# The 64-row step of the products with w_in on both halves of the PE array

## The chip, the cores and the metric

The kernel runs on one core of one Trainium2 chip. The metric is the device time of one execution in microseconds (us). Its engines are PE (TensorE, matmul), DVE (VectorE), ACT (ScalarE), POOL (GpSimd) and SP (SyncE, which issues most DMAs here); each works through its own list of instructions in order.

## The reference

A transformer block in float32: 2048 tokens, width 448, attention with 16 heads of 28, then a gated MLP with spatial mixing. The change lies in the second half:

```python
h = _layernorm(x) * (1 + cb) + sb          # 2048 x 448
z = _gelu(h @ w_in)                        # 448 -> 1792
z1 = z[..., :896]
z2 = _layernorm(z[..., 896:])
g = w_sp @ z2 + b_sp[:, None]              # w_sp 2048 x 2048
x = x + gb * ((z1 * g) @ w_out)            # w_out 896 x 448
```

## The kernel before

All large products use values split into a high and a low part: high = the value rounded to the PE's fast 32-bit format, low = the rest, and a product is high x high + high x low + low x high. The contraction over 448 is cut into three chunks of 128 rows and one of 64. Operands are kept as slots: 0 to 2 are the high parts of the three chunks, 3 to 5 the low parts. The last chunk needs only 64 rows, so its slot 6 holds the high part in rows 0 to 63 and, on the activations' side, the low part in rows 64 to 127; on the weights' side slot 6 holds the high part twice. One full step (6, 6) thus gives high x high and low x high of the last chunk. High x low is left, step (6, 7): the weights' slot 7 holds the low part in rows 0 to 63 and zeros in rows 64 to 127. `STEPS` lists the 11 steps of a product.

After attention, the output projection (`wo_tile`) and the second layernorm give four groups of 512 tokens. For group g, `h2_group(g)` transposes the normalised rows on PE (`ln_transpose`: 16 transposes into four PSUM banks, then ACT writes the scaled value and its high part, DVE the low part) into `h2T[g]`. Then:

- **z1**: `z1_unit(g, f)` is one product of 11 matmuls, 512 tokens wide, for one of 7 blocks f of 128 columns; 28 units, group after group. Gelu on ACT goes from PSUM into one of four slices of `z1t`, and SP stores it to DRAM. Between the units `h2_group(2)`, `h2_group(3)` and the preparation of the other half of w_in (`win_prep`, into `w2`) are issued by a list of positions.
- **z2**: `z2_gemm(t)` for each of 16 token tiles: two products of 11 matmuls, 448 wide; gelu into `zg` (three buffers), statistics on DVE (`bn_stats`, `bn_aggr`), and the reciprocal deviation on POOL (`rstd_of`, two small instructions, lines 106 and 107). One tile later `z2_norm(t)` normalises on DVE (line 825), takes the high part on ACT and the low part on POOL (line 83 is the helper `sub`), and so releases `zg`. During tiles 7 to 10 the first four blocks of w_sp are loaded and split (`wsp_load`).
- **mix**: for each block `tb` of 512 output tokens, 16 steps `st` over the z2 tiles: `mix_part` adds three matmuls into each of 7 accumulators. Blocks of w_sp are loaded ahead by `wsp_load` (SP, then ACT for the high part, DVE for the low part). In the first block w_out is prepared too (`wout_part`: SP, POOL, ACT, POOL). Ahead of all this SP loads `bt` (`b_load`).

PSUM has 8 banks; 7 form the ring from which `bank()` takes a product's accumulator. SBUF pools are opened and closed stage by stage, later ones in the memory of earlier ones: `t3` and `t3b` until the end of z1, `tz` (with `zg`) in z2, `t4` (with `bt`) in the mix; `wp` holds the blocks of w_sp. The instructions of each engine are issued in the order of the program text.

Of the kernel before, what the change touches and what calls it, by code (L numbers as in the profile page):

```python
# [8 lines left out]
F32 = mybir.dt.float32  # L9
F32R = mybir.dt.float32r  # L10
AF = mybir.ActivationFunctionType
# [5 lines left out]
S, D, H, DH, FH = 2048, 448, 16, 28, 896  # L17
EPS = 1e-5
SCALE = DH ** -0.5
NT = S // 128  # L20
NG = 4

# [6 lines left out]
STEPS = STEPS_MAIN + STEPS_Z  # L29
NST = len(STEPS)  # L30
# [3 lines left out]
def tile_adaln_mha_gmlp(ctx, tc, x, wqkv, wo, w_in, w_spT, b_sp, w_out, cT, w_mod, out):  # L34
    nc = tc.nc
    ctx.enter_context(tc.manual_schedule())
    pe, dve, act, pool, sp = nc.tensor, nc.vector, nc.scalar, nc.gpsimd, nc.sync
# [9 lines left out]
    z1_scr = scr.tile([FH, S], F32, name="z1_scr")  # L47
# [8 lines left out]
    cols = {}  # L56
# [25 lines left out]
    def sub(eng, dst, a, hi):  # L82
        eng.tensor_tensor(out=dst, in0=a, in1=hi.bitcast(F32), op=ALU.subtract)  # L83
# [5 lines left out]
    def weight_part(dst, i, raw, hi_eng, lo_eng, zero=True):  # L89

        n = raw.shape[-1]
        h = dst[:, i if i < 3 else 6, 0:n]
        if hi_eng is act:
            act.activation(h, raw, AF.Copy)
        else:
            hi_eng.tensor_copy(h, raw)
        if i < 3:
            sub(lo_eng, dst[:, 3 + i, 0:n], raw, h)
        else:
            sub(lo_eng, dst[0:64, 7, 0:n], raw[0:64], h[0:64])  # L100
            if zero:
                pool.memset(dst[64:128, 7, 0:n].bitcast(F32), 0.0)

    def rstd_of(var, rs, n):

        pool.tensor_scalar(out=rs, in0=var, scalar1=EPS, scalar2=None, op0=ALU.add)
        pool.tensor_tensor(out=rs, in0=rs, in1=mhalf[:, :n], op=ALU.pow)

    def ln_transpose(xns, full_pool, dsts, scol, bcol, engs, los=(pool,) * 4, mid=None, after=None):
# [51 lines left out]
    def bank(name):  # L161
        return ring.tile([128, 512], F32, name=name, tag="s")
# [130 lines left out]
    xns = ln_norm(0)  # L293
# [36 lines left out]
    xns = ln_norm(1)  # L330
    for g in range(NG):
# [46 lines left out]
        if g + 2 < NG:  # L378
            ln_stats(g + 2)
            xns = ln_norm(g + 2)  # L380
# [185 lines left out]
    done = [0]  # L566

    def m_first():
        j, kb = first[done[0]]
# [11 lines left out]
    for u in range(NU + 1):  # L581
        for fn, a in events.pop(u, []):
            fn(*a)
        j = u + LEAD
# [25 lines left out]
    w1 = hview(heapA, 0, 8, 896)  # L610
    h2T = [hview(heapB, g * 3584, 7, 512) for g in range(2)]
# [23 lines left out]
    x3 = {}  # L635
# [27 lines left out]
    def h2_norm(g):  # L663
        mv, rs, _ = mv3.pop(g)
        for tt in range(4):
            xt = x3[4 * g + tt]
            for o, i in ((xt[:, D:], xt[:, 384:D]), (xt[:, :D], xt[:, :D])):
                dve.tensor_scalar(
                    out=o, in0=i, scalar1=mv[:, tt, 0:1], scalar2=rs[:, tt : tt + 1], op0=ALU.subtract, op1=ALU.mult
                )  # L670

    raw_in = {}

    def win_load(i, p):
        raw_in[1, i] = raw = p.tile([128, 896], F32, name="raw_in", bufs=1)
        if i < 3:
            sp.dma_start(raw, w_in[i * 128 : (i + 1) * 128, FH : 2 * FH])
        else:
            load_z(sp, raw, w_in[384:448, FH : 2 * FH])

    def win_prep(half, i, lo_eng):
        weight_part(w2 if half else w1, i, raw_in.pop((half, i)), act, lo_eng)

    def wo_tile(t):
        wo_mm(t, STEPS)
# [17 lines left out]
    h = H - 1  # L703
# [29 lines left out]
    def h2_group(g, after=None):  # L733
        if g >= 2:
            heaps.append(fh.tile([128, 4 * 896], F32R, name="heap", tag=("heapE", "heapC")[g - 2]))
            h2T.append(hview(heaps[-1], 0, 7, 512))
        xns = [x3.pop(4 * g + t) for t in range(4)]
        ln_transpose(xns, t3b, h2T[g], cols["cb"], cols["sb"], (act,) * 4, (dve,) * 4, None, after)

    zbuf = []  # L740

    def z1_unit(g, f):
        ps_t = bank("z1_ps")
        for j, (a, b) in enumerate(STEPS):
            pe.matmul(ps_t, w1[:, b, f * 128 : (f + 1) * 128], h2T[g][:, a, :], start=j == 0, stop=j == NST - 1)  # L745
        if not zbuf:
            zbuf.append(t3.tile([128, 4, 512], F32, name="z1t", tag="x3", bufs=3))
        zt = zbuf[0][:, (7 * g + f) % 4, :]
        act.activation(zt, ps_t, AF.Gelu_apprx_tanh)
        sp.dma_start(z1_scr[f * 128 : (f + 1) * 128, g * 512 : (g + 1) * 512], zt)  # L750

    for t in range(8, 12):
        wo_tile(t)
# [13 lines left out]
    h2_stats(3)  # L767
    win_load(0, t3)
    win_load(1, t3b)
    for g in range(NG):  # L770
        for f in range(7):
            z1_unit(g, f)
            if g == 0 and f == 4:
                h2_group(2)
                h2_norm(3)
            if g == 1 and f == 2:
                h2_group(3)
            if g == 1 and f in (3, 5):
                win_prep(1, f // 4, dve)
                win_load(2 + f // 4, (t3, t3b)[f // 4])  # L780
            if g == 2 and f in (3, 5):
                win_prep(1, 2 + f // 4, dve)
    ph3.close()

    wp = ctx.enter_context(tc.tile_pool(name="wp", bufs=2))
    wsp = {}
    seq = [(tb, st) for tb in range(NG) for st in range(NT)]

    def wsp_load(i):
        tb, st = seq[i]  # L790
        raw = wp.tile([128, 512], F32, name="raw_sp")
        sp.dma_start(raw, w_spT[st * 128 : (st + 1) * 128, tb * 512 : (tb + 1) * 512])
        hi = wp.tile([128, 512], F32R, name="wsp_h", bufs=4)
        act.activation(hi, raw, AF.Copy)  # L794
# [6 lines left out]
    zg = {}  # L801
    z_mv = {}

    def z2_gemm(t):
        g, tt = divmod(t, 4)
        zg[t] = tz.tile([128, FH], F32, name="zg", bufs=3)
        st = tz.tile([128, 2, 6], F32, name="stz")
        for hf in range(2):
            ps_t = bank("z2_ps")
            for j, (a, b) in enumerate(STEPS):  # L810
                pe.matmul(  # L811
                    ps_t[:, :D], h2T[g][:, a, tt * 128 : (tt + 1) * 128], w2[:, b, hf * D : (hf + 1) * D], start=j == 0, stop=j == NST - 1
                )
            act.activation(zg[t][:, hf * D : (hf + 1) * D], ps_t[:, :D], AF.Gelu_apprx_tanh)
            dve.bn_stats(out=st[:, hf, :], in_=zg[t][:, hf * D : (hf + 1) * D])
        mv = tz.tile([128, 2], F32, name="mvz")
        dve.bn_aggr(out=mv, in_=st)
        rs = tz.tile([128, 1], F32, name="rsz")
        rstd_of(mv[:, 1:2], rs, 1)
        z_mv[t] = (mv, rs)  # L820

    def z2_norm(t):
        mv, rs = z_mv.pop(t)
        z = zg.pop(t)
        dve.tensor_scalar(out=z, in0=z, scalar1=mv[:, 0:1], scalar2=rs, op0=ALU.subtract, op1=ALU.mult)
        act.activation(z2[t][:, 0, :], z, AF.Copy)
# [25 lines left out]
    def mix_part(tb, st, f):  # L852
        hi, lo = wsp[tb, st]
        if st == 0:
            acc[f] = bank("acc")
        fs = slice(f * 128, (f + 1) * 128)
        pe.matmul(acc[f], z2[st][:, 0, fs], hi, start=st == 0, stop=False)  # L857
        pe.matmul(acc[f], z2[st][:, 0, fs], lo, start=False, stop=False)  # L858
        pe.matmul(acc[f], z2[st][:, 1, fs], hi, start=False, stop=st == NT - 1)  # L859

    bt = {}
    z1s = {}
# [111 lines left out]
```

## Time and profile before

| | |
|---|---|
| time, median of 3 runs | 1457.15 us (1454.2 to 1459.6) |
| profiled execution, its own time | 1459.32 us |
| its span, first to last instruction | 1457.5 us |
| busy share PE, DVE, ACT, POOL | 98%, 61%, 50%, 19% |
| z1 products, in the trace | from 934.0 to 1007.4 us |
| z2 products | from 1007.4 to 1078.7 us |

The profile is that of one execution. "L811" is a line of the kernel. A row of the timeline has the start and the length in us, the engine, the line, the operation, output and inputs with their shapes, the number of instructions merged, and in brackets how long the engine had been idle and what it had waited for. PE's weight loads stand under PEld, and a small q behind an engine marks its queue's own work such as the issue of a DMA.

### The profile page before, as it was taken

The numbers are of one execution on the slowest core, as the hardware profiler recorded it, in microseconds if no ns is written. First come the engines' busy times: TensorE is split into PE (matmuls) and PEld (weight loads), VectorE is DVE, ScalarE is ACT, GpSimd is POOL, SyncE is SP. The second block draws the span as 40 slices with busy tenths as digits, with TensorE's granted clock in tenths as the row PEclk, the third lists the DMA queues.
The fourth block names the chain that finished last, engine by engine and source line by source line (L and its number), as shares of the span: only waits on it lengthen the run. The fifth ranks groups of instructions, "written<-read, shape, count | busy, mean of one in ns | idle before, by whom it ended". The sixth has DMA issues, their size and how long they took to land.

```text
span 1457.5 us, 19648 instructions
## 1 busy us (share of the span) xinstructions
PE 1431.1 (98%) x7314; PEld 1010.2 (69%) x7314; DVE 887.4 (61%) x1462; ACT 731.1 (50%) x1390; POOL 282.6 (19%) x257
## 2 busy tenths in 40 slices
PE   6899999999999999999999999999999999999998
PEld 5788755555555555555555556888988888888887
DVE  6567888888888888888888832921542411414114
ACT  3523577777767777776776786452432210211111
POOL 5853200000002021001000022100663400302002
PEclk9999999999999999999999999999999999999999
DMA  7454402221022212222032003432003322323223
GB/s 215 135 158 167 154 2 54 53 47 41 21 53 54 49 35 49 54 49 56 28 78 53 11 18 124 156 120 94 15 22 98 120 76 66 110 65 98 84 69 107
DMA packets 56183, 111.44 MB, mean 76 GB/s; under 512 B 11926, under 2 KB 22806, under 8 KB 53542
## 3 DMA queue, kind: packets, MB, share of 16 engines
q1 hardware_dynamic: 55962, 110.03, 25.8%
q8 instruction: 57, 0.93, 0.3%
q14 instruction: 38, 0.31, 0.1%
q10 hardware_dynamic: 126, 0.17, 0.1%
HBM read 75.89 MB, written 29.48 MB: 72 GB/s over the span
## 4 chain that ended last, share of the span: by engine, by line
PE 91%; DVE 3%; DMA 3%; POOL 2%; issue 1%; ACT 0%; SPq 0%; DVEq 0%; ACTq 0%; POOLq 0%
PE st_ps L441 18%; PE o_ps L456 16%; PE mt L410 16%; PE acc L857 7%; PE acc L859 7%; PE acc L858 7%; PE z_ps L811 5%; PE z_ps L745 5%; PE pq L280 4%; PE y_ps L898 2%; PE y_ps L897 2%; PE y_ps L899 2%; PE pv L271 1%; PE wo_ps L627 1%; DVE acc L216 1%
## 5 line engine op out<-in xcount | busy, mean ns | idle before, releaser
L415 DVE TENSOR_REDUCE pm<-mt 128x1 f32<-128x512 f32 x1024 | 631.5, 680 | 115.9 <-PE mt L410 115.6
L445 ACT ACTIVATE P<-st_ps 128x512 f32<-128x512 f32 x1024 | 513.1, 620 | 151.4 <-PE st_ps L441 151.1
L441 PE MATMUL st_ps<-qst,kst 128*128 128x512 f32 x1024 | 408.1, 409 | 0.5 <-DMA qst<-nl 0.4
L410 PE MATMUL mt<-kst,qst 128*128 128x512 f32 x1024 | 403.0, 394 | 0.3 <-DVE pm L415 0.3
L441 PEld LDWEIGHTS st_ps<-qst,kst 128*128 128x128 f32 x1024 | 191.0, 187 | 150.1 <-issue 82.2
L456 PE MATMUL o_ps<-P,V 128*32 128x512 f32 x2048 | 247.2, 598 | 0.0
L410 PEld LDWEIGHTS mt<-kst,qst 128*128 128x128 f32 x1024 | 192.5, 188 | 33.9 <-DVE pm L415 0.7
L83 DVE TENSOR_TENSOR wsp_l<-raw_sp,wsp_h 128x512 fp32r<-128x512 f32 x64 | 50.6, 794 | 188.5 <-ACT wsp_h L794 188.5
L794 ACT ACTIVATE wsp_h<-raw_sp 128x512 fp32r<-128x512 f32 x64 | 40.2, 631 | 232.3 <-DMA raw_sp<-in_w_spT_dram 183.4
L456 PEld LDWEIGHTS o_ps<-P,V 128*32 128x32 f32 x2048 | 54.1, 109 | 123.7 <-issue 114.7
L83 POOL TENSOR_TENSOR heapF<-u,heapD 128x512 fp32r<-128x512 f32 x27 | 44.6, 1686 | 256.5 <-ACT heapD L876 256.5
L482 POOL TENSOR_TENSOR osb<-osb,rb 128x512 f32<-128x512 f32 x15 | 19.2, 1282 | 363.7 <-DMA rb<-r_scr 309.1
L857 PE MATMUL acc<-wsp_h,heapD 128*128 128x512 f32 x224 | 87.6, 391 | 0.8 <-DVE u L874 0.7
L859 PE MATMUL acc<-wsp_h,heapD 128*128 128x512 f32 x224 | 87.3, 390 | 0.0
L858 PE MATMUL acc<-wsp_l,heapD 128*128 128x512 f32 x224 | 87.2, 389 | 0.0
L280 PE MATMUL pq<-heapD 128*128 128x512 f32 x196 | 61.9, 392 | 0.0
L83 POOL TENSOR_TENSOR nl<-nf,nh 16x128 fp32r<-16x128 f32 x16 | 7.2, 452 | 266.7 <-issue 140.2
L902 DVE TENSOR_TENSOR x2t<-x2t,y_ps 128x448 f32<-128x448 f32 x12 | 7.5, 621 | 73.5 <-PE y_ps L899 73.5
L282 ACT ACTIVATE qf<-pq 128x512 f32<-128x512 f32 x28 | 16.7, 595 | 66.3 <-PE pq L280 66.3
L857 PEld LDWEIGHTS acc<-wsp_h,heapD 128*128 128x128 f32 x224 | 42.0, 188 | 10.0 <-DVE u L874 1.8
L859 PEld LDWEIGHTS acc<-wsp_h,heapD 128*128 128x128 f32 x224 | 42.0, 188 | 9.0
L858 PEld LDWEIGHTS acc<-wsp_l,heapD 128*128 128x128 f32 x224 | 42.1, 188 | 8.3
(164 smaller groups left out, 1766.6 us busy)
## 6 DMA issues: line engine op xcount, KB each, us to landing
raw_sp<-in_w_spT_dram SPq DMA_DIRECT2D x64, 256.0 KB
kst<-qk_scr SPq DMA_DIRECT2D x45, 224.0 KB
qst<-qk_scr SPq DMA_DIRECT2D x45, 224.0 KB
qk_scr<-qh SPq DMA_DIRECT2D x28, 256.0 KB
qk_scr<-ql SPq DMA_DIRECT2D x28, 256.0 KB
z_scr<-z1t SPq DMA_DIRECT2D x28, 256.0 KB
z<-z_scr SPq DMA_DIRECT2D x28, 256.0 KB
wm<-in_w_mod_dram SPq DMA_DIRECT2D x12, 392.0 KB
```

Of the source, the lines that this page charges most:

```text
L83: eng.tensor_tensor(out=dst, in0=a, in1=hi.bitcast(F32), op=ALU.subtract)
L280: pe.matmul(pq, wqk[:, b, m * 128 : (m + 1) * 128], hT[g][:, a, :], start=j == 0, stop=j == NST - 1)
L410: pe.matmul(mt, qst[h % 3][:, t * 128 : (t + 1) * 128], kst[h % 3][:, kb * 512 : (kb + 1) * 512], start=True, stop=True)
L415: dve.tensor_reduce(out=pms[h][:, t, kb : kb + 1], in_=mt, axis=AX.X, op=ALU.max)
L441: pe.matmul(st, kst[h % 3][:, kt * 128 : (kt + 1) * 128], qst[h % 3][:, qb * 512 : (qb + 1) * 512], start=True, stop=True)
L445: act.activation(p, st, AF.Exp, scale=SCALE)
L456: pe.matmul(otile[h][32 * qb : 32 * qb + 32, :], V[:, kt, h, :], ptiles.pop((u, qb)), start=kt == 0, stop=kt == NT - 1)
L745: pe.matmul(ps_t, w1[:, b, f * 128 : (f + 1) * 128], h2T[g][:, a, :], start=j == 0, stop=j == NST - 1)
L811: pe.matmul(ps_t[:, :D], h2T[g][:, a, tt * 128 : (tt + 1) * 128], w2[:, b, hf * D : (hf + 1) * D], start=j == 0, stop=j == NST - 1)
L857: pe.matmul(acc[f], z2[st][:, 0, fs], hi, start=st == 0, stop=False)
L858: pe.matmul(acc[f], z2[st][:, 0, fs], lo, start=False, stop=False)
L859: pe.matmul(acc[f], z2[st][:, 1, fs], hi, start=False, stop=st == NT - 1)
```

## The change

Products with w_in are issued in batches. In a batch every unit first gets its 10 full steps, each unit in its own PSUM bank. Then come the last steps (6, 7) of all units, now with 64 rows each: units of an even group take rows 0 to 63, units of an odd group rows 64 to 127, alternately. For that the weights' slot 7 holds the low part in both halves (no zeros), and for odd groups `h2T`'s slot 6 holds the low part in rows 0 to 63 and the high part in rows 64 to 127. Gelu of a batch follows its last steps.

z1 runs in batches of 4, 4 and 6 units over groups 0 and 1, then the same over groups 2 and 3. z2 takes two tiles at a time, one of an even and one of an odd group, four units to a batch; the tiles' order becomes 0, 4, 1, 5, 2, 6, 3, 7, 8, 12, and so on, and the mix goes through z2 and w_sp in that order. `zg` has four buffers, and `z2_norm` of a pair follows the next pair's products. `h2_group(2)`, `h2_group(3)` and `win_prep` are issued within batches, after a unit's ten steps.

```diff
@@ weight_part, with zero=None for w_in
-            sub(lo_eng, dst[0:64, 7, 0:n], raw[0:64], h[0:64])
+            rows = slice(0, 128 if zero is None else 64)
+            sub(lo_eng, dst[rows, 7, 0:n], raw[rows], h[rows])
...
+    HALF = (slice(0, 64), slice(64, 128))
+
+    def pair_units(units, finish):
+        pss = []
+        for a, b, p in units:
+            pss.append(bank("z_ps")[:, : p[1]])
+            for j, (x, y) in enumerate(STEPS[:-1]):
+                pe.matmul(pss[-1], a(x, y, slice(0, 128)), b(x, y, slice(0, 128)), start=j == 0, stop=False)
+            p[0]()
+        x, y = STEPS[-1]
+        for i, (a, b, p) in enumerate(units):
+            pe.matmul(pss[i], a(x, y, HALF[i % 2]), b(x, y, HALF[i % 2]), start=False, stop=True)
+        for i, ps_t in enumerate(pss):
+            finish(i, ps_t)
...
@@ ln_transpose; h2_group passes HALF[1 - g % 2] as zlo
-                sub(los[c], hi[64:128], f[64:128], hi[64:128])
+                sub(los[c], hi[zlo], f[zlo], hi[zlo])
...
+    def z1_after(g, f):
+        if (g, f) == (0, 2):
+            h2_group(2)
+            h2_norm(3)
+        if (g, f) == (1, 4):
+            h2_group(3)
+        for i, u in enumerate(((0, 5), (0, 6), (2, 2), (3, 3))):
+            if (g, f) == u:
+                win_prep(1, i, dve)
+                if i < 2:
+                    win_load(2 + i, (t3, t3b)[i])
+
+    for gs in ((0, 1), (2, 3)):
+        for fs in ((0, 1), (2, 3), (4, 5, 6)):
+            z1_units(gs, fs)
...
+    order = [t for g in (0, 2) for tt in range(4) for t in (4 * g + tt, 4 * g + 4 + tt)]
...
+    def z2_pair(ts):
+        st = {}
+        for t in ts:
+            zg[t] = tz.tile([128, FH], F32, name="zg", bufs=4)
+            st[t] = tz.tile([128, 2, 6], F32, name="stz", bufs=4)
+        seq = [(t, hf) for hf in range(2) for t in ts]
...
+        def finish(i, ps_t):
+            t, hf = seq[i]
+            act.activation(zg[t][:, hf * D : (hf + 1) * D], ps_t, AF.Gelu_apprx_tanh)
+            dve.bn_stats(out=st[t][:, hf, :], in_=zg[t][:, hf * D : (hf + 1) * D])
+
+        pair_units([unit(t, hf) for t, hf in seq], finish)
+        for t in ts:
+            mv = tz.tile([128, 2], F32, name="mvz", bufs=4)
+            dve.bn_aggr(out=mv, in_=st[t])
+            rs = tz.tile([128, 1], F32, name="rsz", bufs=4)
+            rstd_of(mv[:, 1:2], rs, 1)
+            z_mv[t] = (mv, rs)
...
-    for t in range(NT + 1):
-        if t < NT:
-            z2_gemm(t)
-        if t > 0:
-            z2_norm(t - 1)
-        if 7 <= t < 11:
-            wsp_load(t - 7)
+    for i in range(9):
+        if i < 8:
+            z2_pair(order[2 * i : 2 * i + 2])
+        if i > 0:
+            for t in order[2 * i - 2 : 2 * i]:
+                z2_norm(t)
+        if i in (4, 5):
+            wsp_load(2 * i - 8)
+            wsp_load(2 * i - 7)
```

More of the change, by code (lines that the diff above doesn't have):

```diff
@@ L107, in rstd_of, with ln_transpose @@
         pool.tensor_tensor(out=rs, in0=rs, in1=mhalf[:, :n], op=ALU.pow)
-    def ln_transpose(xns, full_pool, dsts, scol, bcol, engs, los=(pool,) * 4, mid=None, after=None):
+    def ln_transpose(xns, full_pool, dsts, scol, bcol, engs, los=(pool,) * 4, mid=None, after=None, zlo=slice(64, 128)):
         tps = []
@@ L565, in tile_adaln_mha_gmlp @@
     first = first + [(t, kb) for t in range(NT, LEAD) for kb in range(4)]
-    done = [0]
+    done = [0, 0]
     def m_first():
@@ L681, in win_prep @@
     def win_prep(half, i, lo_eng):
-        weight_part(w2 if half else w1, i, raw_in.pop((half, i)), act, lo_eng)
+        weight_part(w2 if half else w1, i, raw_in.pop((half, i)), act, lo_eng, None)
     def wo_tile(t):
@@ L737, in h2_group, with z1_units, unit @@
         xns = [x3.pop(4 * g + t) for t in range(4)]
-        ln_transpose(xns, t3b, h2T[g], cols["cb"], cols["sb"], (act,) * 4, (dve,) * 4, None, after)
+        ln_transpose(xns, t3b, h2T[g], cols["cb"], cols["sb"], (act,) * 4, (dve,) * 4, None, after, HALF[1 - g % 2])
     zbuf = []
[L742 to L750, printed above, removed]
+    def z1_units(gs, fs):
+        seq = [(g, f) for f in fs for g in gs]
+        def unit(g, f):
+            return (
+                lambda x, y, rows: w1[rows, y, f * 128 : (f + 1) * 128],
+                lambda x, y, rows: h2T[g][rows, x, :],
+                (lambda: z1_after(g, f), 512),
+            )
+        def finish(i, ps_t):
+            g, f = seq[i]
+            if not zbuf:
+                zbuf.append(t3.tile([128, 4, 512], F32, name="z1t", tag="x3", bufs=3))
+            zt = zbuf[0][:, done[1] % 4, :]
+            done[1] += 1
+            act.activation(zt, ps_t, AF.Gelu_apprx_tanh)
+            sp.dma_start(z1_scr[f * 128 : (f + 1) * 128, g * 512 : (g + 1) * 512], zt)
+        pair_units([unit(g, f) for g, f in seq], finish)
     for t in range(8, 12):
@@ L769, in tile_adaln_mha_gmlp @@
     win_load(1, t3b)
[L770 to L782, printed above, removed]
+    def z1_after(g, f):
[12 more added lines that the diff above has]
+            z1_units(gs, fs)
     ph3.close()
@@ L791, in wsp_load @@
         raw = wp.tile([128, 512], F32, name="raw_sp")
[L792 removed]
+        sp.dma_start(raw, w_spT[order[st] * 128 : (order[st] + 1) * 128, tb * 512 : (tb + 1) * 512])
         hi = wp.tile([128, 512], F32R, name="wsp_h", bufs=4)
@@ L802, in tile_adaln_mha_gmlp, with unit, finish @@
     z_mv = {}
[L804 to L820, printed above, removed]
+    def z2_pair(ts):
[4 more added lines that the diff above has]
+        seq = [(t, hf) for hf in range(2) for t in ts]
+        def unit(t, hf):
+            g, tt = divmod(t, 4)
+            return (
+                lambda x, y, rows: h2T[g][rows, x, tt * 128 : (tt + 1) * 128],
+                lambda x, y, rows: w2[rows, y, hf * D : (hf + 1) * D],
+                (lambda: None, D),
+            )
+        def finish(i, ps_t):
+            t, hf = seq[i]
[8 more added lines that the diff above has]
+            z_mv[t] = (mv, rs)
     def z2_norm(t):
@@ L856, in mix_part @@
         fs = slice(f * 128, (f + 1) * 128)
-        pe.matmul(acc[f], z2[st][:, 0, fs], hi, start=st == 0, stop=False)
-        pe.matmul(acc[f], z2[st][:, 0, fs], lo, start=False, stop=False)
-        pe.matmul(acc[f], z2[st][:, 1, fs], hi, start=False, stop=st == NT - 1)
+        pe.matmul(acc[f], z2[order[st]][:, 0, fs], hi, start=st == 0, stop=False)
+        pe.matmul(acc[f], z2[order[st]][:, 0, fs], lo, start=False, stop=False)
+        pe.matmul(acc[f], z2[order[st]][:, 1, fs], hi, start=False, stop=st == NT - 1)
     bt = {}
```

## The prediction

> **What bounds the kernel now.** I read the page's busy table and chain first, then the stages that the change touches.
>
> ```profile
> span 1457.5 us, 19648 instructions
> PE 1431.1 (98%) x7314; PEld 1010.2 (69%) x7314; DVE 887.4 (61%) x1462; ACT 731.1 (50%) x1390; POOL 282.6 (19%) x257
> PE 91%; DVE 3%; DMA 3%; POOL 2%; issue 1%; ACT 0%; SPq 0%; DVEq 0%; ACTq 0%; POOLq 0%
> ```
>
> PE carries the chain, so a matmul taken away is time gained, as long as nothing else becomes late. Next, the busy time by stage (us, then PE, PEld, DVE, ACT, POOL): the z1 products, then the z2 products.
>
> ```profile
> 934.00:1007.40 73.40, 73.40 (x342) 61.23 (x341) 24.42 (x50) 34.95 (x55) 3.38 (x5) 1.00 0.36 129
> 1007.40:1078.60 71.20, 71.20 (x353) 65.99 (x352) 38.12 (x63) 29.27 (x48) 43.34 (x41) 1.00 0.06 19
> ```
>
> Both are bound by PE without a gap. But the page's 19% for POOL hides that in z2 POOL is busy 43.34 of 71.20 us, 61%; that matters below. The spacing of matmuls, not their 0.39 us duration, is what one costs: from the view of line 745 and from the chain in order of time:
>
> ```profile
> L745 PE MATMUL z_ps<-heap,heapA x154: 389/389/389, 972.5 to 1007.2; 128*128 128x512 f32 x154
> 1007.54 71.34 PE z_ps L811 x352
> ```
>
> z1: 34.7/153 = 0.227 us each; z2: 71.34/352 = 0.203 us.
>
> **The change part by part. 1: the halves on PE.** Sixty full matmuls (28 in z1, 32 in z2) become sixty half-height ones, issued in fourteen bursts (z1: four of 4 and two of 6; z2: eight of 4). If the two of a pair run side by side, 30 spacings vanish: 14 x 0.227 + 16 x 0.203 = 6.4 us. That is the ceiling. No half-height matmul is in this trace. The nearest rows are attention's products on a quarter of the columns, four side by side, between full ones (PE's timeline, with two rows of its weight loads):
>
> ```profile
> 602.32 0.40 PE L410 MATMUL mt<-kst,qst 128*128 128x512 f32 x1
> 602.64 1.92 PE L456 MATMUL o_ps<-P,V 128*32 128x512 f32 x16
> 603.10 0.13 PEld L456 LDWEIGHTS o_ps<-P,V 128*32 128x32 f32 x4 [0.30 <-issue]
> 603.53 0.13 PEld L456 LDWEIGHTS o_ps<-P,V 128*32 128x32 f32 x4 [0.30 <-issue]
> 604.50 0.50 PE L441 MATMUL st_ps<-qst,kst 128*128 128x512 f32 x1
> 604.83 0.39 PE L410 MATMUL mt<-kst,qst 128*128 128x512 f32 x1
> ```
>
> From full to part the start is 0.32 us later instead of 0.23: +0.09. Coming back, the first full record is 0.50 long instead of 0.39 and the next starts after 0.33: +0.10. Between, sixteen parts take 1.86 us where four groups, whose weight loads start 0.43 apart, would take 1.72: +0.14. So a round trip costs 0.33 us with small weights; the weights here have all 128 columns, whose load lies bare on the way back (+0.11) and will on the way in too, so I take 0.41. [...]
>
> A burst of 4 in z1: 2 x 0.227 + 0.41 = 0.86 against 4 x 0.227 = 0.91; of 6: 1.09 against 1.36. Sum over z1: 4 x 0.04 + 2 x 0.27 = 0.7 us gained. In z2: 2 x 0.203 + 0.41 = 0.82 against 0.81: nothing. Bounds: 6.4 us gained (no drain), or 14 x 0.41 = 5.7 us lost (halves in file, each a full spacing).
>
> **2: the second h2T group is needed earlier.** z1 took seven products of group 0 first; now its second product reads group 1.
>
> ```profile
> 934.00 12.66 PE L745 MATMUL z_ps<-heapB,heapA 128*128 128x512 f32 x55
> 938.59 0.69 DVE L83 TENSOR_TENSOR heapB<-hfull,heapB 64x512 fp32r<-64x512 f32 x1
> ```
>
> The first unit's ten matmuls end at 936.27, and the second's tenth, which reads the last chunk, would start at 938.31. That chunk is ready at 939.28. A wait of 1.0 us; the other chunks come in time. The later groups keep their places (after 5 and 10 units), and group 3, needed at unit 16 instead of 22, still has five units, 11 us, between its transposes and its first use. z1 as a whole: -0.7 + 1.0 = +0.3 us.
>
> **3: z2's normalisation in pairs.** Here I see the price. z2's gelu writes `zg`; a buffer of `zg` comes free when POOL has subtracted (z2's low part). There were three buffers for tiles in flight singly; now there are four for two pairs, so the gelu of pair i waits for the subtractions of pair i-2, which POOL does only after the rstd of pair i-1. From the timelines of ACT, DVE and POOL in z2:
>
> ```profile
> 1040.03 0.21 DVE L817 BATCH_NORM_AGGREGATE mvz<-stz 128x2 f32<-128x12 f32 x1
> 1040.15 0.69 DVE L825 TENSOR_SCALAR zg<-zg,mvz,rsz 128x896 f32<-128x896 f32 x1
> 1040.32 0.60 POOL L106 TENSOR_SCALAR rsz<-mvz 128x1 f32<-128x1 f32 x1 [0.67 <-DVE mvz L817]
> 1041.01 0.57 POOL L107 TENSOR_TENSOR rsz<-rsz,mhalf 128x1 f32<-128x1 f32 x1
> 1041.97 2.13 POOL L83 TENSOR_TENSOR heapD<-zg,heapD 128x896 fp32r<-128x896 f32 x1 [0.39 <-ACT heapD L826]
> 1013.72 0.23 POOL L106 TENSOR_SCALAR rsz<-mvz 128x1 f32<-128x1 f32 x1 [64.11 <-DMA raw_sp<-in_w_spT_dram]
> 1046.90 2.19 DVE L83 TENSOR_TENSOR wsp_l<-raw_sp,wsp_h 128x512 fp32r<-128x512 f32 x1 [1.60 <-ACT wsp_h L794]
> 1076.57 0.96 ACT L814 ACTIVATE zg<-z_ps 128x448 f32<-128x448 f32 x2
> 1077.12 1.15 DVE L815 BATCH_NORM_STATS2 stz<-zg 128x6 f32<-128x448 f32 x2 [1.51 <-ACT zg L814]
> ```
>
> POOL's tiny L106 takes 0.23 us alone and 0.60 beside DVE's L825, ending just behind it: they exclude each other. [...]
>
> The loop of one pair, from the moment the second tile's buffer is free: three gelus 0.42 apart, the last done at 1.4; statistics 0.53 apart, the last done at 2.3; two aggregates, 2.65; two rstd on POOL (0.6 + 0.6 for the first, whose second step now meets the second L825, 0.3 + 0.6 for the other, and gaps of 0.1), 5.2; two subtractions of 2.13, about 9.4 us. PE delivers a pair every 40 x 0.203 + 0.82 = 8.9 us. So each pair falls back 0.5 us: 0.6 at pair 2, five more times 0.5, and about 1.6 for the four `wsp` splits that DVE now does two by two behind POOL's subtractions (2.19 instead of 0.69): 4.7 us at the last pair. PE doesn't feel it within z2: of seven banks three are spare, so a late gelu has three units, 6 us.
>
> **4: where it lands.** When z2 ends, the spatial mix begins:
>
> ```profile
> 1010.57 0.55 ACT L814 ACTIVATE zg<-z_ps 128x448 f32<-128x448 f32 x1 [2.35 <-DMA z_scr<-z1t]
> 1078.72 0.39 PE L857 MATMUL acc<-wsp_h,heapD 128*128 128x512 f32 x1
> 1084.20 4.45 POOL L83 TENSOR_TENSOR heapB<-zg,heapB 128x896 fp32r<-128x896 f32 x2 [0.39 <-ACT heapB L826]
> 1088.67 0.33 SPq L866 DMA_DIRECT2D bt<-in_b_sp_dram  x1
> 1093.09 1.15 POOL L846 TENSOR_TENSOR raw_out<-raw_out,bc_gb 128x448 f32<-128x448 f32 x1 [4.45 <-DMA raw_out<-in_w_out_dram]
> 1094.76 0.61 ACT L794 ACTIVATE wsp_h<-raw_sp 128x512 fp32r<-128x512 f32 x1
> 1095.41 1.23 DVE L83 TENSOR_TENSOR wsp_l<-raw_sp,wsp_h 128x512 fp32r<-128x512 f32 x1 [10.82 <-ACT wsp_h L794]
> ```
>
> SP's load of `bt`, in memory that z2's pool gave back, goes out 0.02 us after POOL's last subtraction (1088.65), and behind it in SP's order the fifth `w_sp` block. That a new pool waits for the whole old one is seen at 1010.57, where z2's first gelu waited for z1's last store. The block's low part is ready at 1096.64, 8.0 us after the last subtraction. PE needs it in the fifth step of the mix: 1078.72 + 84 x 0.227 + 0.23 = 1098.0. So the slack today is 1.35 us.
>
> With the change the last pair's second gelu could start at 1078.9 and starts 4.7 us late, 1083.6; one loop later, 1093.1, the subtractions of pair 6 are done, then two more: 1097.7, with z1's 0.3 us 1098.0. That is 9.35 us later than today, less 1.35 of slack: **+8.0 us**. Some 2.6 us of it show already in the first mix step, whose banks the late gelus hold; they are no addition.
>
> PE then idles some 5 us in the fifth step. Such a gap occurs once already (PE's timeline, then the windows with granted clock):
>
> ```profile
> 72.71 4.00 PE L271 MATMUL pv<-wv,heapD 128*128 128x448 f32 x11 [4.49 <-DVE V L273]
> 66.00:73.30 7.30, 2.81 (x14) 2.25 (x13) 7.23 (x6) 3.88 (x6) 7.27 (x4) 1.00 1.00 256
> 73.30:76.70 3.40, 3.40 (x11) 3.05 (x10) 0.42 (x1) 0.00 (x0) 1.28 (x1) 0.50 0.63 157
> ```
>
> After 4.49 us without a matmul the clock was at 0.50 for 3.4 us, 1.7 us lost. Here the wait is broken by one matmul (the high part arrives first), so 0 to 1.7; I take 0.9.
>
> **Sum.** Steps 1 and 2 in z1 are inside the 8.0. Total +8.9: from the profiled execution's 1459.32 us (span 1457.5) 1468.2; from the median 1457.15, which is 2.2 below it, **1466.2 us**.
>
> Nothing else is priced: the low part over 128 rows is one instruction as before; `win_prep` sits at the same unit numbers; gelus in bursts wait for z1t's four slices, but the next product's banks are ready before.
>
> **Rivals.**
> The tail stays hidden (not slower). If POOL's rstd slips between DVE's two L825 without waiting, it takes 2.0 instead of 2.6 us and the subtraction follows at once: a loop of about 8.6 us, below PE's 8.9, no lag. The last subtraction ends near 1092.4, and 2.5 us remain: 1459.6. It decides at a loop of 8.9. For it: one L106 did take 0.23. Against: fifteen others stood beside an L825. If SP's queue isn't held by the last subtraction either, z1's +0.3 remains: 1457.5.
>
> The halves don't overlap (the change not doing what it says): z1 gains nothing and loses 6 x 0.41 + 1.0 = 3.5, and the loop starts that much later: +3.2, 1469.4. Nothing in the trace shows two row groups at once; for overlap speak the column groups of L456.
>
> [...]
>
> The loop is worse: if each rstd step waits out both L825, it is about 10 us, and the total +14: 1471.
>
> **How the numbers follow.** 0.5%, 7.3 us, is about what a measurement of this kernel can tell from no change: 1449.9 and 1464.4. Forecast 0.50, of which 0.08 lie below 1464.4; halves in file 0.13; worse loop 0.09; tail hidden 0.19; no drain 0.06, with tail hidden 0.03, of which a third beyond 0.5%. Slower 0.42 + 0.13 + 0.09 = 0.64; faster 0.01, raised to 0.03 for what I overlook; same 0.33. The range leaves out the half of the hidden tail nearest to no change and the extreme loop: 1459 to 1472.5.
>
> **What would show it.** Right: half matmuls starting in pairs some ns apart; a gap of 0.2 to 0.4 us around each burst; a wait of 1 us near 938; the second gelu of a pair waiting for POOL's L83, more with each pair; the last z2 subtraction near 1098 with `bt` right behind; PE idle in the fifth mix step. Wrong, if that subtraction ends before 1090, or halves start a full spacing apart, or PE waits inside z2.

## The result and the profile after

| | before | after |
|---|---|---|
| time, median of 6 runs | 1455.68 us (1453.64 to 1459.60) | 1464.35 us (1463.42 to 1466.06) |
| ratio after / before, 95% interval | | 1.0066 [1.0052, 1.0079] |
| profiled execution, its own time | 1459.32 us | 1465.81 us |
| its span | 1457.5 us | 1464.0 us |

The change makes the kernel 8.7 us slower. The page of the changed kernel (span; busy time, share and instructions of each engine; the chain's shares by engine):

```profile
span 1464.0 us, 19631 instructions
PE 1433.2 (98%) x7314; PEld 1002.6 (68%) x7314; DVE 889.7 (61%) x1462; ACT 729.8 (50%) x1390; POOL 282.5 (19%) x255
PE 86%; DVE 4%; POOL 4%; issue 2%; DMA 2%; ACT 1%; SPq 0%; DVEq 0%; POOLq 0%; ACTq 0%
```

The busy table has hardly moved; the chain has: PE's share fell from 91% to 86%, since from 1031.3 to 1102.0 us it now runs through ACT, DVE, POOL and a load in place of PE. Where the time went is seen by stage. The windows of z1, z2 and the start of the mix (start to start of the sixth mix step) in the kernel after, then that last window in the kernel before (length; busy time of PE, PEld, DVE, ACT and POOL, each with its count; granted clock; DMA share; GB/s):

```profile
931.23:1004.54 73.31, 73.01 (x341) 57.47 (x339) 23.65 (x49) 30.92 (x50) 2.53 (x4) 1.00 0.32 111
1004.54:1076.15 71.61, 71.61 (x355) 61.85 (x353) 34.34 (x58) 29.33 (x50) 38.33 (x39) 1.00 0.11 37
1076.15:1108.96 32.81, 27.59 (x107) 21.36 (x106) 9.01 (x12) 8.55 (x13) 20.23 (x14) 0.90 0.14 47
```

```profile
1078.72:1102.53 23.81, 23.81 (x106) 19.71 (x105) 5.47 (x8) 6.04 (x9) 13.37 (x12) 1.00 0.20 64
```

z1 takes 73.31 us instead of 73.38 and z2 71.61 instead of 71.34 (first matmul to first matmul): the sixty halves bring nothing that counts. The first five mix steps take 32.81 us instead of 23.81: +9.0. PE is idle there for 5.2 us, and the granted clock is 0.90 on average.

The start of z1 is not a fixed point: it lies at 934.0 us in the profiled execution of the kernel before, at 931.2 in that of the kernel after, and between 926.5 and 931.3 in those of the experiments, whose text ahead of z1 is the same. So stages are compared here from z1's start on. From there to the end it is 523.5 us before and 532.8 after, +9.3. From the sixth mix step to the end nothing differs: 355.0 and 355.1.

### The profile page after: what moved, and what is told of

It is laid out like the page before. It is cut to its first block, busy times and chain, and to the rows that moved or that the text cites. A ratio compares the mean times of both kernels' runs of the same rounds, so it can differ in the third digit from the quotient of the medians.

```text
span 1464.0 us, 19631 instructions
## 1 busy us (share of the span) xinstructions
PE 1433.2 (98%) x7314; PEld 1002.6 (68%) x7314; DVE 889.7 (61%) x1462; ACT 729.8 (50%) x1390; POOL 282.5 (19%) x255
## 4 chain that ended last, share of the span: by engine, by line
PE 86%; DVE 4%; POOL 4%; issue 2%; DMA 2%; ACT 1%; SPq 0%; DVEq 0%; POOLq 0%; ACTq 0%
PE st_ps L460 18%; PE o_ps L475 16%; PE mt L429 16%; PE acc L904 6%; PE acc L903 6%; PE acc L905 6%; PE z_ps L115 6%; PE pq L299 4%; PE y_ps L944 2%; PE y_ps L943 2%; PE y_ps L945 2%; POOL heapD L85 1%; PE wo_ps L646 1%; PE pv L290 1%; DVE stz L856 1%
## 5 line engine op out<-in xcount | busy, mean ns | idle before, releaser
L85 DVE TENSOR_TENSOR wsp_l<-raw_sp,wsp_h 128x512 fp32r<-128x512 f32 x64 | 53.7, 844 | 184.8 <-ACT wsp_h L828 184.8
L903 PEld LDWEIGHTS acc<-wsp_h,heapD 128*128 128x128 f32 x224 | 42.7, 191 | 16.5 <-ACT wsp_h L828 4.1
L856 DVE BATCH_NORM_STATS2 stz<-zg 128x6 f32<-128x448 f32 x32 | 18.0, 614 | 57.3 <-DMA raw_sp<-in_w_spT_dram 29.2
```

Of the source, the lines that this page charges most:

```text
L903: pe.matmul(acc[f], z2[order[st]][:, 0, fs], hi, start=st == 0, stop=False)
```

## The experiments

**Theory A** is the prediction's: POOL's loop in z2 falls behind PE; the last subtraction frees z2's pool late; `bt`, and behind it in SP's order the fifth block of w_sp, go out late; PE waits in the fifth mix step. **Rival B**: PE itself loses around the bursts: what the expectations call drains is the time beyond the usual spacings that it takes from full to half-height matmuls and back, 0.41 us a burst by the estimate in part 1 of the prediction and 14 x 0.41 = 5.7 us in all. **Rival C**: gelus that come four at a time hold PSUM banks when the mix wants them, and that alone costs the time.

### e1: bt and w_out behind the blocks of w_sp

```diff
-    b_load(0)                  # ahead of the mix loops
...
+        if tb == 0:            # behind the block's first 14 steps
+            b_load(0)
         for f in range(2):
             z1_load(tb, f)
...
-            if tb == 0 and st % 2 == 0:
-                wout_part(st // 2)
+            if tb == 0 and st in (3, 5, 7, 9, 11, 12, 13):
+                wout_part((3, 5, 7, 9, 11, 12, 13).index(st))
```

> The load of bt is moved behind the first 14 steps of the mix and the preparation of w_out to its steps 3 to 13, so no block of w_sp stands behind work that waits for POOL's last z2 subtraction. Theory A (POOL's chain in z2 ends late, the loads behind it come late, PE waits in the fifth mix step and its clock halves): the wait of some 5 us in the fifth step and the half clock vanish; left are +0.2 us up to the mix and 1.4 us of bank waits in its first step, so about +1.6 us on the kernel before, 1457.3. The last subtraction still ends about 17.9 us after the mix begins. Rival B (the price is PE's: drains and weight loads around the half-height matmuls): no change, about +8.7, 1464.4. Rival C (gelus in bursts hold the PSUM banks): the bank waits are the price, also about 1464.

1454.98 us against 1453.34; ratio 1.0012 [1.0001, 1.0024]. The last subtraction on POOL's timeline, and the window from the mix's first matmul to the sixth step:

```profile
1088.84 2.57 POOL L85 TENSOR_TENSOR heapB<-zg,heapB 128x896 fp32r<-128x896 f32 x1
1072.60:1098.20 25.60, 24.51 (x108) 19.66 (x107) 12.96 (x14) 8.55 (x13) 18.45 (x12) 1.00 0.15 50
```

POOL is as late as ever: its last subtraction ends 18.8 us after the mix starts (after: 17.9; before: 9.9). But 7.2 of the 9.0 us are gone, and the clock stays at 1.00. The late loop costs by what stands behind the load that waits for it: the fifth block and w_out's first part. This edit moves `bt` and w_out's parts at once, so how the 7.2 us divide between the two was not measured. The 1.8 us left in the window are mostly the one wait of a mix bank for a late gelu: 1.49 us from start to start instead of 0.23. So held banks are worth 1.3 to 1.8 us and not the whole, and e2 shows that they go too when the gelus come on time.

### e2: z2_norm of a pair ahead of the next pair's products

```diff
     for i in range(9):
-        if i < 8:
-            z2_pair(order[2 * i : 2 * i + 2])
         if i > 0:
             for t in order[2 * i - 2 : 2 * i]:
                 z2_norm(t)
+        if i < 8:
+            z2_pair(order[2 * i : 2 * i + 2])
```

> Each pair's z2_norm is issued right behind its own products instead of behind the next pair's, nothing else. Theory A: POOL subtracts a pair before the next pair's rstd, no gelu waits for a zg buffer, the last subtraction ends about 11 us after the mix begins instead of 17.9, the fifth step waits 0 to 1 us, the clock stays full: +0.2 to +1.2 us, about 1456.4. Rival B: no change, about 1464.4. Rival C: the gelus still come four at a time, so if bursts alone held the banks, the waits in the first mix step (1.4 us) would stay; by theory A they go, since the gelus come on time.

1455.11 us against 1453.34; ratio 1.0008 [0.9998, 1.0018]. The last pair on the timelines of ACT, POOL and SP:

```profile
1071.64 1.85 ACT L855 ACTIVATE zg<-z_ps 128x448 f32<-128x448 f32 x4 [2.02 <-PE z_ps L119]
1074.62 0.22 POOL L125 TENSOR_SCALAR rsz<-mvz 128x1 f32<-128x1 f32 x1 [1.94 <-DVE mvz L861]
1079.48 2.13 POOL L85 TENSOR_TENSOR heapB<-zg,heapB 128x896 fp32r<-128x896 f32 x1
1081.64 0.33 SPq L912 DMA_DIRECT2D bt<-in_b_sp_dram  x1
```

Here a pair is normalised as soon as its statistics are there, so the next pair's gelus find free buffers: the four of the last pair run in a row and wait for PE alone. L125 takes 0.22 us again, where it took 0.70 in the kernel after. The last subtraction ends 9.93 us after the mix starts, as in the kernel before, the five steps take 23.91 us, and from z1's start to the end it is 524.3 (+0.8). The bursts on PE, the four gelus at a time and the halves are all still there. So neither B nor C carries the time: the text order of `z2_norm` does.

### e3: the halves replaced by full steps

```diff
-            pe.matmul(pss[i], a(x, y, HALF[i % 2]), b(x, y, HALF[i % 2]), start=False, stop=True)
+            pe.matmul(pss[i], a(x, y, slice(0, 128)), b(x, y, slice(0, 128)), start=False, stop=True)
```

> The last step of each unit takes all 128 rows again (it then adds low x low of the last chunk as well), in the same batches. Theory A: the halves save 0.04 us in a burst of 4 and 0.25 in one of 6 of z1 and nothing in z2, so this is 0.7 us slower up to the mix, and since POOL's chain sets the end, about +9.3 on the kernel before, 1465. Rival B: without the drains it is faster than the changed kernel by what they cost, up to 5.7 us: 1459. If the halves had been worth their 6.4 us, it would be 1470.

1464.25 us against 1453.34; ratio 1.0072 [1.0058, 1.0087]. The windows of z1 and z2:

```profile
926.53:1000.93 74.40, 73.78 (x342) 61.14 (x340) 24.04 (x50) 31.90 (x52) 2.54 (x4) 1.00 0.32 109
1000.93:1072.27 71.34, 71.34 (x354) 66.11 (x353) 34.36 (x58) 28.75 (x49) 38.35 (x39) 1.00 0.10 37
```

There is no half-height matmul left (the full step also adds low x low of the last chunk), and the loss stays. B falls. The windows also weigh the halves by themselves. In z1 PE is busy for 73.78 us here; in e4, whose z1 is that of the change and has the same 0.62 us idle, for 73.11: the halves gain 0.67 us. In z2 they cost 0.27 (71.61 against 71.34), though the bursts themselves break even there (step 1 below): the full steps between them are 0.2038 us apart instead of 0.2027, which over some 300 of them is about the difference. Why was not followed up.

### e4: z1 of the change, z2 and mix of the kernel before

```diff
-    order = [t for g in (0, 2) for tt in range(4) for t in (4 * g + tt, 4 * g + 4 + tt)]
+    order = list(range(NT))
...
-    def z2_pair(ts):           # and its loop
+    def z2_gemm(t):            # and its loop, as before
```

> The changed z1 (batches and halves) with the z2 stage and the mix order of the kernel before (its last steps take all 128 rows, adding low x low). Theory A: +0.3 us, 1456, with 1.0 us of wait in the first z1 batch and no wait in the mix. Rival B: z1 has six of the fourteen bursts, so 3 to 4 us of the 8.7 should show here: 1459.5. Rival C: z1's bursts wait for the z1t slices and banks, some us.

1453.97 us against 1453.34; ratio 1.0002 [0.9990, 1.0014]. z1 takes 73.73 us, z2 71.44, the five mix steps 23.80 as before. All of the loss sits in z2's part of the change, and what z1 gains by its halves (0.67) it gives back in the wait for the second group of `h2T`: 0.87 us beyond the usual spacing in this run.

### e5: one rstd for the two tiles of a pair

```diff
-        for t in ts:
-            mv = tz.tile([128, 2], F32, name="mvz", bufs=4)
-            dve.bn_aggr(out=mv, in_=st[t])
-            rs = tz.tile([128, 1], F32, name="rsz", bufs=4)
-            rstd_of(mv[:, 1:2], rs, 1)
...
+        mv = tz.tile([128, 2, 2], F32, name="mvz", bufs=2)
+        for k, t in enumerate(ts):
+            dve.bn_aggr(out=mv[:, k, :], in_=st[t])
+        rs = tz.tile([128, 2], F32, name="rsz", bufs=2)
+        rstd_of(mv[:, :, 1], rs, 2)
```

> The changed kernel with one rstd for a pair (two POOL instructions on two columns instead of four on one), so that only POOL's part of the loop is shortened. Theory A: the loop of a pair falls from 9.24 us to about 8.2, below PE's 8.91, so no gelu is late, the last subtraction ends about 13 us after the mix begins instead of 17.9, PE waits some 2 us in the fifth mix step and the clock stays full: about +2.2 us on the kernel before. If the loop were not POOL's (but that of ACT or of the banks), nothing would change: +8.7.

1460.58 us against 1455.85; ratio 1.0034 [1.0021, 1.0047]. That shortens POOL's loop and changes nothing else. POOL's timeline, the first rstd step of four pairs, then PE's in the fifth mix step:

```profile
1039.83 0.60 POOL L125 TENSOR_SCALAR rsz<-mvz 128x2 f32<-128x2 f32 x1 [2.99 <-DVE mvz L861]
1048.74 0.60 POOL L125 TENSOR_SCALAR rsz<-mvz 128x2 f32<-128x2 f32 x1 [2.99 <-DVE mvz L861]
1058.12 0.60 POOL L125 TENSOR_SCALAR rsz<-mvz 128x2 f32<-128x2 f32 x1 [2.99 <-DVE mvz L861]
1067.48 0.60 POOL L125 TENSOR_SCALAR rsz<-mvz 128x2 f32<-128x2 f32 x1 [3.00 <-DVE mvz L861]
...
1094.09 0.57 PE L904 MATMUL acc<-wsp_h,heapD 128*128 128x512 f32 x1 [2.22 <-ACT wsp_h L828]
1095.34 0.80 PE L905 MATMUL acc<-wsp_l,heapD 128*128 128x512 f32 x1 [0.68 <-DVE wsp_l L85]
```

The direction is A's, the size was missed: 4.7 us by the times where 2.2 were expected. The lag is nearly gone. A turn takes 8.91 us, which is PE's own pace, and 9.37 in the two pairs with splits of w_sp, so 0.9 us are left of it. Still the last subtraction ends 14.3 us after the mix starts (before 9.9, after 17.9): this rest is not lag but order, since behind the last pair's gelus POOL has two pairs to subtract. PE's waits fell to 2.4 and 1.0 us from start to start, less a spacing each. But the clock still falls behind them, for 6.8 us as in the kernel after (0.89 on average over the window, the matmuls 0.43 us apart), and of the window's 6.4 us above before (30.2 against 23.8) that is the 2.9 which the waits and the way out of the last burst (0.1) don't explain. The expectation had said that the clock stays full.

### e6: the wait filled with idle matmuls

```diff
+            if tb == 0 and st == 4:
+                wu2 = ps_o.tile([128, 512], F32, name="wu2", tag="o")
+                for _ in range(20):
+                    pe.matmul(wu2[:, 0:128], ones, ones, start=True, stop=True)
```

> The changed kernel with 20 small matmuls on constants into an unused bank ahead of the fifth mix step, some 4 us of PE work where PE waits anyway. Theory A: the blocks of w_sp come as late as before, but PE isn't idle long enough for its clock to be halved, so the 2.4 us that the half clock costs after the wait are saved: about +6.5 us on the kernel before. If the half clock cost nothing, +8.7 or more.

1463.54 us against 1455.85; ratio 1.0059 [1.0043, 1.0074]. PE's timeline in the fifth mix step (the trace shows two records for each of the 20 small matmuls), and where the fourth block of tokens begins:

```profile
1093.86 4.62 PE L959 MATMUL wu<-ones 128*128 128x128 f32 x40
1098.24 0.47 PE L903 MATMUL acc<-wsp_h,heapD 128*128 128x512 f32 x1
...
1099.60 0.40 PE L905 MATMUL acc<-wsp_h,heapD 128*128 128x512 f32 x1
...
1348.31 0.50 PE L903 MATMUL acc<-wsp_h,heapD 128*128 128x512 f32 x1 [0.74 <-DVE u L920]
```

With PE kept busy the clock stayed full (1.00 in the window of the five steps, and 0.40 us a matmul where the kernel after has 0.63), and the five steps take 30.90 us instead of 32.81: the half clock was worth 1.9 us there, and if anything more, since the block's low part comes 0.3 us later in this run, counted from the mix's start. By the time of the run that can't be seen: 1.4 us return between the sixth step and the end (356.42 against 355.06), most of them because at the start of the fourth block PE waits twice for `gate` (DVE's L920, as in the row at 1348.31; 1.1 us each from start to start) where the kernel after waits once. Why that second wait appears was not followed up. By time, inconclusive; by the window, the clock's part is shown.

### e7: e1, e2 and e5 together, and the first batch of z1 in group order

```diff
         seq = [(g, f) for f in fs for g in gs]
+        if gs[0] == 0 and fs[0] == 0:
+            seq = [(g, f) for g in gs for f in fs]   # last steps still alternate
```

> The changed kernel with loads first, norm at once, one rstd for a pair, and the first z1 batch taking both units of group 0 ahead of those of group 1. Theory A: nothing waits any more; the halves' own gain in z1 is left: z1 to mix 0.7 us shorter than in the kernel before, the mix as before: -0.7 us, not to be told from no change by the time, but by the trace from z1's start to the end (522.8 instead of 523.5 us). If the halves had a hidden price, it would be above the kernel before.

1454.68 us against 1455.85; ratio 0.9996 [0.9987, 1.0005]. The three windows:

```profile
927.45:1000.17 72.72, 72.72 (x342) 57.56 (x340) 24.05 (x50) 31.28 (x51) 2.53 (x4) 1.00 0.32 112
1000.17:1071.77 71.60, 71.60 (x354) 61.85 (x352) 29.30 (x60) 30.58 (x53) 35.98 (x28) 1.00 0.13 45
1071.77:1095.68 23.91, 23.91 (x107) 19.82 (x106) 7.32 (x12) 6.50 (x11) 9.76 (x8) 1.00 0.16 53
```

PE is busy without a gap in all three. With the wait for `h2T` gone z1 is 0.66 us shorter than before, z2 0.26 longer, and the sum from z1's start to the end 0.3 shorter (523.2). That is all that the halves have to give in this form, and no measurement of this kernel tells it from nothing.

### e8: z2 in batches of six units

Batches of 3, 3, 3, 3, 2 and 2 pairs of units, each normalised at once, with one rstd for two tiles and the loads of e1, so that there are fewer bursts to pay 0.41 us for.

```diff
+    for b, n in enumerate((3, 3, 3, 3, 2, 2)):
+        z2_units([u for pr in allu[at_ : at_ + n] for u in pr])
```

> As the run with all repairs, and z2 in batches of 6, 6, 6, 6, 4, 4 units instead of eight of 4, so that two round trips into the half-height mode are saved. By the price of 0.41 us for one, z2 becomes 0.8 us shorter: -1.5 us on the kernel before, 522.0 us from z1's start to the end. If six banks held at a time make PE wait for gelus, that shows at the start of a batch and takes the gain back.

1461.50 us against 1455.85; ratio 1.0045 [1.0033, 1.0057]; from z1's start to the end 529.0 us, where 522.0 was expected. PE's timeline at the start of the last batch, and a window on the clock:

```profile
1071.59 0.37 PE L115 MATMUL z_ps<-heapF,heap 128*128 128x448 f32 x1
1073.74 0.88 PE L115 MATMUL z_ps<-heapD,heap 128*128 128x448 f32 x3 [1.78 <-ACT zg L861]
...
1075.30:1078.70 3.40, 3.40 (x11) 2.08 (x10) 3.40 (x6) 0.00 (x0) 0.77 (x1) 0.50 0.39 142
```

Six units take six of the ring's seven banks, so the next batch has one bank until gelus return the others. PE waited inside z2 (2.15 us from start to start) and again 3.2 us in the first mix step, with 3.4 us of half clock between. This is C's mechanism, but not by the size of the batch alone: the gelus that hold the banks stand in ACT's order behind the high parts of the pair before, and for those ACT had waited 5.29 and 5.97 us for DVE's normalisation (its L882 at 1070.43 and 1080.96). In e7, with four units to a batch, the same order makes PE wait nowhere.

### e9: e4 with the first batch of z1 in group order

> The changed z1 alone (z2 and the mix order as before, last steps of z2 over 128 rows, adding low x low), with the first z1 batch taking both units of group 0 first. Theory A: z1 is 0.7 us shorter than in the kernel before (72.7 instead of 73.4 us), z2 and the mix as before: 522.9 us from z1's start to the end instead of 523.5, and a ratio of about 0.9995, which the times can't tell from 1. If the halves in z1 cost something elsewhere, it is above 1.

1454.84 us against 1454.73; ratio 0.9995 [0.9986, 1.0004]. z1 takes 72.72 us, without a gap, against 73.38 before; the first five mix steps are those of before. But the 0.7 us gained in z1 don't reach the end: from z1's start on it is 523.6 us, where 522.9 was expected and the kernel before has 523.5. z2 is 0.1 longer and the stretch behind the sixth mix step 0.6 (355.6 against 355.0); whether that is chance or a price of the change was not settled, and the times resolve neither. So no version here beats the kernel before by a measurable amount.

## Why the prediction was right, step by step

**Step 1, the halves on PE: right to some hundredths.** PE's timeline of the kernel after at z1's start and around the first burst:

```profile
931.23 4.49 PE L115 MATMUL z_ps<-heapB,heapA 128*128 128x512 f32 x19
936.02 5.05 PE L115 MATMUL z_ps<-heapB,heapA 128*128 128x512 f32 x21 [0.30 <-DVE heapB L85]
941.01 0.73 PE L119 MATMUL z_ps<-heapB,heapA 64*128 64x512 f32 x4
941.67 0.73 PE L115 MATMUL z_ps<-heapB,heapA 128*128 128x512 f32 x2
```

The single records inside read: last full step 940.689; halves 941.007 and 941.011, 941.342 and 941.346; next full steps 941.668 and 942.007. A pair starts 4 ns apart, so the halves do overlap. But the first pair starts 0.32 us behind the full step, the second 0.33 behind the first, and the way back costs 0.33 and 0.34. From last full step to the second full one behind it are 1.318 us; less two spacings of 0.227 the burst costs 0.86, as predicted. The burst of six costs 1.09, predicted 1.09; the burst of four in z2 0.81, predicted 0.82. What makes PE start later there no run shows; the records give the sizes. The 0.41 us beside the work are 0.09 on the way in, 0.11 at the second pair, and 0.10 and 0.11 on the way back. The prediction has the same 0.41, but doesn't show how its 0.33 becomes it, so that the hundredths agree is in part luck.

**Step 2, the wait for the second h2T group: right in kind.** It is there, behind the nineteenth matmul: 0.69 us from start to start in this run, which is 0.46 beyond the usual spacing, and 0.87 beyond it in e1, e4 and e6, where 1.0 was predicted. z1 as a whole came out within 0.4 us of before in all of them.

**Step 3, POOL's loop: right, the lag 1.1 us too large.** POOL's timeline, one loop of z2, then ACT's second to fourth gelu of five pairs:

```profile
1034.48 0.70 POOL L125 TENSOR_SCALAR rsz<-mvz 128x1 f32<-128x1 f32 x1 [2.49 <-DVE mvz L861]
1035.26 0.97 POOL L126 TENSOR_TENSOR rsz<-rsz,mhalf 128x1 f32<-128x1 f32 x1
1036.21 0.22 POOL L125 TENSOR_SCALAR rsz<-mvz 128x1 f32<-128x1 f32 x1
...
1037.05 4.18 POOL L85 TENSOR_TENSOR heapD<-zg,heapD 128x896 fp32r<-128x896 f32 x2
1043.72 0.70 POOL L125 TENSOR_SCALAR rsz<-mvz 128x1 f32<-128x1 f32 x1 [2.49 <-DVE mvz L861]
...
1041.27 1.42 ACT L855 ACTIVATE zg<-z_ps 128x448 f32<-128x448 f32 x3 [0.41 <-POOL heapD L85]
1050.52 1.42 ACT L855 ACTIVATE zg<-z_ps 128x448 f32<-128x448 f32 x3 [0.76 <-POOL heapD L85]
1060.22 1.42 ACT L855 ACTIVATE zg<-z_ps 128x448 f32<-128x448 f32 x3 [1.56 <-POOL heapD L85]
1070.29 1.42 ACT L855 ACTIVATE zg<-z_ps 128x448 f32<-128x448 f32 x3 [1.98 <-POOL heapB L85]
1079.90 1.42 ACT L855 ACTIVATE zg<-z_ps 128x448 f32<-128x448 f32 x3 [1.53 <-POOL heapB L85]
```

Read the loop downwards: rstd waits for the aggregate of DVE, whose statistics wait for the gelus; the subtractions follow; and the next pair's second gelu starts when the second of them has ended (1037.05 + 4.18 = 1041.23, gelu at 1041.27). One turn takes 1043.72 - 1034.48 = 9.24 us, where 9.4 was worked out, against PE's 8.91. Both rstd steps of the first tile run long beside L869 of DVE (0.70 and 0.97 instead of 0.23 and 0.57). In the kernel before each of the fifteen L106 of z2 that ran beside an L825 took 0.59 to 0.61 us and ended 0.07 to 0.09 behind it, and the sixteenth, alone, took 0.23; that is the measured ground of the prediction's reading that the two exclude each other, and how they come to, no run shows. In the two pairs with splits of w_sp a turn takes 10.08. So the lag is 6 x 0.33 + 2 x 0.84 = 3.7 us, not 4.7: the mis-sized term is the excess of a turn, 0.33 instead of 0.5. In the trace the last pair's second gelu, which could start at 1076.3, starts at 1079.90. PE doesn't wait inside z2, as predicted: its window is busy from end to end.

**Step 4, where it lands: the place is right, and the chain but for its last link; the wait was over-sized, the clock under-sized.** POOL, SP, ACT, DVE and PE around the fifth mix step:

```profile
1091.90 2.11 POOL L85 TENSOR_TENSOR heapB<-zg,heapB 128x896 fp32r<-128x896 f32 x1
1094.04 0.33 SPq L912 DMA_DIRECT2D bt<-in_b_sp_dram  x1
1098.46 1.13 POOL L892 TENSOR_TENSOR raw_out<-raw_out,bc_gb 128x448 f32<-128x448 f32 x1 [4.45 <-DMA raw_out<-in_w_out_dram]
1099.62 0.58 ACT L893 ACTIVATE heap<-raw_out 128x448 fp32r<-128x448 f32 x1 [10.70 <-POOL raw_out L892]
1100.11 0.61 ACT L828 ACTIVATE wsp_h<-raw_sp 128x512 fp32r<-128x512 f32 x1
1100.75 1.21 DVE L85 TENSOR_TENSOR wsp_l<-raw_sp,wsp_h 128x512 fp32r<-128x512 f32 x1 [12.87 <-ACT wsp_h L828]
1080.50 0.50 PE L903 MATMUL acc<-wsp_h,heapD 128*128 128x512 f32 x1 [1.10 <-ACT zg L855]
...
1100.77 0.80 PE L903 MATMUL acc<-wsp_h,heapD 128*128 128x512 f32 x1 [3.66 <-ACT wsp_h L828]
1102.02 0.80 PE L904 MATMUL acc<-wsp_l,heapD 128*128 128x512 f32 x1 [0.45 <-DVE wsp_l L85]
1102.61 0.63 PE L905 MATMUL acc<-wsp_h,heapD 128*128 128x512 f32 x1
```

The last subtraction ends at 1094.01, `bt` goes out 0.03 us later, and the fifth block's low part is ready at 1101.96, 7.95 us after the subtraction (predicted 8.0). Measured from the mix's start the subtraction ends at 17.86 us instead of 9.93, 7.9 later: 3.7 of it lag, 4.2 the two pairs that POOL subtracts behind the last gelus. 9.05 was predicted, and of the 1.1 between 1.0 is the lag's. Less the slack of 1.35 that makes 6.6 us, and PE's waits add up to it: about 1.7 in the first mix step (mostly the bank at 1080.50; predicted 2.6), then from start to start, less a spacing of 0.227 each, 3.82 for the block's high part and 1.02 for its low part.

The last link isn't the block's own load. ACT takes the block's high part at 1100.11, straight behind the high part of w_out's first part (L893), for which it had waited on POOL's scaling (L892) and that on its own load behind `bt`. The first row of the windows below has a DMA share of 0.00 from 1099 us on, so the block had landed at least 1.1 us before ACT took it. The kernel before has the same order (its rows at 1093.09 and 1094.76), so the 8 us and the sum stand, but they are more than the time of a load.

The clock is the other mis-sized term. The window in which nothing is loaded, then those before and in the half clock:

```profile
1099.00:1102.00 3.00, 0.80 (x1) 0.29 (x1) 1.21 (x1) 1.09 (x2) 1.73 (x2) 0.67 0.00 0
1096.72:1100.03 3.31, 0.39 (x2) 0.00 (x0) 0.00 (x0) 0.41 (x1) 1.13 (x1) 1.00 0.43 146
1100.03:1106.86 6.83, 5.64 (x12) 4.13 (x13) 1.90 (x2) 1.45 (x4) 2.74 (x2) 0.50 0.24 77
```

A range of 0 to 1.7 us was given and 0.9 taken, on the reading that a broken wait costs at most what an unbroken one did. Instead the clock stood at 0.50 for 6.8 us, twice the 3.4 of the example before. Behind the last wait one spacing is 0.59 us and ten are 0.427, where 0.227 is usual: 0.36 + 10 x 0.20 = 2.4 us, which with the 6.6 makes the window's 9.0. e6, which avoids it, saves 1.9. So the two misses, 1.4 us too much wait and 1.5 us too little clock, cancel: +9.3 from z1's start in the trace and +8.7 by the times, against +8.9. That the total comes so close is luck; the place and the direction are not. The absolute forecast stands 1.9 us above the result: 1.5 of it is the median of the kernel before, which later runs put at 1455.68, 0.15 a slip in the forecast's sum (1457.15 + 8.9 is 1466.05 and not 1466.2), and 0.2 the change itself.

**The rivals.** That the tail stays hidden would have needed a loop below 8.9 us; e2 makes one by another order, and the time returns to that of before. That the halves don't overlap is contradicted by the records of the bursts, where the two of a pair start 1 to 9 ns apart, and so is the "no drain" of the chances: no run shows a burst that pays nothing on its way in and out, and 0.41 us stood there instead. The worse loop, about 10 us, occurs only in the pairs with splits of w_sp.

## What to carry to other kernels

Half-height matmuls on two row groups gained here only what a burst saved beyond its way in and out, 0.41 us: four of them about broke even (0.86 us against 0.91 in z1, 0.81 against 0.81 in z2) and six gained a quarter of a microsecond (1.09 against 1.36), so count units per burst before rearranging a loop for it. When a loop is put into pairs, walk round the cycle of its buffers once (gelu, statistics, reciprocal, subtraction, buffer free) and compare its turn with the bottleneck engine's: 0.3 us too much per turn, and work put off by a pair, stay hidden until the loop ends and then meet the next stage's first loads. Put the load that waits for a closing pool last in its queue: of the 9.0 us lost, moving it and the preparation of w_out took away 7.2. And ask of every engine behind such a load what stands ahead in its own order: here ACT rounded a part of w_out first, though the block had landed.

## What the runs showed of the hardware that was not expected

- The granted clock fell to 0.50 after waits much shorter than the 4.49 us seen before: after one of 1.78 us in e8 (0.50 for the 3.4 us from 1075.30) and after one of 2.22 in e5. It did not fall after the waits of about 1.1 us at the start of the mix in e1 (1.00 over the five steps) and in the kernel after (1.00 from 1080.50 to 1084.00), nor after one of 1.73 us up to 38.18 in the kernel before (1.00 from there to 42.60), nor after e8's next wait: PE idles 2.80 us in its first five mix steps (27.54 less 24.74), and their mean of 0.98 is what the end of the stretch before leaves. So the length of a wait alone doesn't decide; what does, no run shows.
- The half clock lasted 3.4 us in e8 and in the example at 73.30, where PE was busy right behind the wait, and 6.8 us in the kernel after and in e5, where a second wait of 0.45 and 0.68 us followed within it. No run took that second wait alone away, so that the length hangs on it is a reading of these four cases and not shown.
- Within a burst the second pair of halves starts 0.33 us behind the first and the third 0.24 behind the second (records of the burst of six: 1003.647, 1003.982, 1004.217).
- The wait for `h2T`'s second group comes in two sizes, about 0.46 and 0.87 us beyond the usual spacing, in kernels with the same z1; what decides between them stays open.
